# A gated recurrence and an ELU layer: one sum of the weights' rounding as accumulating transfers, and the weight block sums back in an even row

## The chip, the cores and the metric

The kernel runs on one core of a Trainium2 chip. The metric is the device time of one execution in microseconds (us), lower is better. All engines of the core (PE for matrix products, DVE for elementwise work, ACT for activations and copies out of PSUM, POOL, and SP, which only issues transfers) run their own instruction queues in order and meet through semaphores.

## The reference

```python
# q, k, v, a_re, a_im: (4, 8, 768, 48) float32
mag = np.sqrt(a_re * a_re + a_im * a_im)
scale = np.minimum(mag, 0.999) / (mag + 1e-06)
a_re_n, a_im_n = (a_re * scale, a_im * scale)
for t in range(S):                      # one complex gated state per head
    S_re, S_im = a * S_re - b * S_im + kv[t], a * S_im + b * S_re
    y[:, :, t] = np.einsum('bhd,bhde->bhe', q[:, :, t], S_re)
x = y.transpose(0, 2, 1, 3).reshape(3072, 384)
h = x @ w_in                            # (384, 2048), float64 weights
g = np.where(h > 0.0, h, np.exp(np.minimum(h, 0.0)) - 1.0)
return (g @ w_out).astype(np.float32)   # (2048, 384), float64 weights
```

Here `a, b` stand for `a_re_n, a_im_n` of step `t`. The weights arrive as float64, and the kernel rounds them to float32 itself, on the bits.

## The kernel before, in words

The tokens are cut into 12 units of 256 (two batches by 128 steps). A unit goes through the decays (logarithms, angles, exponentials on ACT and DVE), the recurrence as chunked matrix products, a small regrouping of its result into the layer's input (`seam`, six small transfers `x<-y`), the first layer (w_in) and the second (w_out). Units 0 and 1 compute the layer directly (`inner` L1202, `elu` L1215, `project` L1225). From unit 3 on both layers use fewer products on sums and differences of weight blocks (`mult` L1449, `product` L1299); these block sums are made once on DVE (`summed_in` L1398 for w_in, `combined` L1272 for w_out).

**The order** is written by hand. A list `first` gives the steps of the opening stage one by one. After it, every step has a place on a scale of 16 slots to a unit (`put(at, fn, ...)`), and the steps are issued in order of place. Each engine then works its own queue strictly in that order, so a DVE step put in early delays all DVE steps behind it.

**The weights** are 16 blocks of 768 float32 per partition: `("in", 0)` to `("in", 7)`, which are slices of w_in, 3 rows of 256 per partition, and `("out", 0)` to `("out", 7)`, slices of w_out, 768 in a row. Each is fetched by SP as 768 KB of float64 words into one of two raw buffers and then rounded by five DVE steps. Each entry `(convert,)` of `first` issues one step. The first four are in `_rounded` (L36): two on the high words give a truncated float32 `f` (L40, L43), a third takes the exponent of it into `p` (L46), a fourth scales the low words by that exponent, again into `p` (L50). The fifth is a sum of the two into the weight tile:

```python
        nc.vector.tensor_tensor(out=dst, in0=p, in1=f, op=ALU.add)   # L655
```

`f` and `p` share a ring of two buffers (tag `wt`). The first layer of units 0 and 1 is `inner(u, f)` for f = 0, 2, ..., 14; piece f reads block `("in", f // 2)`. Its PSUM bank comes from a ring of three (tag `mlp`) and becomes free when `elu` (ACT L1219, L1220, then DVE L1221) has read it. `project(u, n, f0, f1)` reads blocks `("out", f0 // 2)` and on.

**Other steps that the change touches.** `carry_back` (L817) fetches a row of turns from DRAM by a POOL transfer, which `carried` (L822, DVE) adds to the angles before the PE product L837 of `turned`. `noted` (L784) takes two DVE reductions for a later check of the inputs. `test_fetch` and `test` (L661, L676) read the weights' high words once more in 48 pieces and reduce each on DVE (L680), for the same check; `verdict` (L1485) and `pronounced` (L1506) conclude it. `product` ends in `done` (L1336), which writes a result tile `o` and sends it out. For units from 4 on there is a DVE step `lengths` (L772) that the PE product L889 waits for, and `slopes` (L780) that ACT's angles (L815) wait for.

Of the kernel before, what the change touches and what calls it, by code (L numbers as in the profile page):

```python
# [16 lines left out]
C = 128  # L17
# [18 lines left out]
def _rounded(nc, w, f, p):  # L36


    lo, hi = w[:, :, 0], w[:, :, 1]
    yield nc.vector.tensor_scalar(  # L40
        out=f, in0=hi, scalar1=LOW, scalar2=3, op0=ALU.bitwise_and, op1=ALU.logical_shift_left
    )
    yield nc.vector.scalar_tensor_tensor(  # L43
        out=f, in0=hi, scalar=TOP, in1=f, op0=ALU.bitwise_and, op1=ALU.bitwise_or
    )
    yield nc.vector.tensor_scalar(  # L46
        out=p, in0=f, scalar1=F32_EXP, scalar2=None, op0=ALU.bitwise_and
    )
    p = p.bitcast(FP32)
    yield nc.vector.scalar_tensor_tensor(  # L50
        out=p, in0=lo, scalar=2.0**-52, in1=p, op0=ALU.mult, op1=ALU.mult
    )
# [453 lines left out]
def kernel(  # L506
# [140 lines left out]
    def rounded(kind, m):  # L647

        w, dst = raw.pop((kind, m))
        f = sb.tile([C, WF * DM], U32, tag="wt", bufs=2, name="wf")  # L650
        p = sb.tile([C, WF * DM], U32, tag="wt", bufs=2, name="wp")
        yield from _rounded(nc, w, f, p)
        n = dst.shape[-1]
        f, p = (x.bitcast(FP32).rearrange("p (b n) -> p b n", n=n) for x in (f, p))
        nc.vector.tensor_tensor(out=dst, in0=p, in1=f, op=ALU.add)  # L655
        done.append((kind, m))
        yield True
# [159 lines left out]
    def carry_back(u):  # L817

        if u in carry and u > 3:
            nc.gpsimd.dma_start(out=flat(nat[u]["e"])[0:1], in_=carry[u])  # L820

    def carried(u):  # L822

        if u in carry:
            row = nat[u]["th"][0:1].rearrange("p n h d -> p (n h d)")
            nc.vector.scalar_tensor_tensor(
                out=row, in0=carry[u] if u < 4 else flat(nat[u]["e"])[0:1], scalar=float(2 * np.pi), in1=row, op0=ALU.mult,
                op1=ALU.add,
            )
# [469 lines left out]
    def product(u, k, h):  # L1299
# [36 lines left out]
        def done(i, n, a, *sums):  # L1336
            if u < NU - 1:
                o = new("o", 2, [C, HN])
            else:
                o = flat(new("S", 8, [C, 1, H, D]))[:, 0:HN]  # L1340
# [28 lines left out]
    def A(r, k):  # L1369

        if r == "t":
            return spare[1][:, ds(12 * C, 4 * C)]
# [23 lines left out]
    ] + SUMS[11:] + [(("t", 0), (1, 1), MINUS, 5)]  # L1396
# [52 lines left out]
    def mult(u, p):  # L1449
# [3 lines left out]
        a = four(A(*(("t", 0) if p == 6 and u == PAIRED + 1 else IN_OF[p])))  # L1453
# [31 lines left out]
    def verdict():  # L1485
# [17 lines left out]
        nat[0]["fit"] = t = work([1, NU + NR])  # L1503
        nc.tensor.matmul(t, lhsT=ones, rhs=fit, start=True, stop=True)

    def pronounced():  # L1506
        t = nat[0]["fit"]
# [62 lines left out]
    def decays_of(u, *at):  # L1570
        fns = squares, joined, logarithms, powers, lengths, ratios, slopes, noted, angles, carried
        if u > 3:
            put(at[4] + 0.05, carry_back, u)
# [4 lines left out]
    def gates_of(u, *at):  # L1578
# [8 lines left out]
        (joined, 0, 0), (squared, "ai", 1), (joined, 0, 1), (logarithms, 0, 0),  # L1587
        (logarithms, 0, 1), (fetch, "in", 1), (fetch, "in", 2), (ratios, 0, 0), (lengths, 0, 0),
        (warm, 2), (warm, 1), (lengths, 0, 1), (sums, 1), *2 * [(convert,)],
        (table, "exp_and_others"), (ratios, 0, 1), (powers, 0, 0), (powers, 0, 1), (warm, 2),  # L1590
        (sums, 0), (warm, 1), (angles, 0, 0), (angles, 0, 1), (summed, 0), (summed, 1),
        (decayed, 0, 0), (turned, 0, 0), (decayed, 0, 1), (turned, 0, 1), (waves, 0, 0),
        (waves, 0, 1), (begun, 1), (warm, 1), (scaled, 0, "q", 0), (ends, 0), (scaled, 0, "k", 0),
        (scaled, 0, "k", 1), (scaled, 0, "q", 1), (warm, 1), (gated, 0, 0), (warm, 1), (noted, 0),
        (table, "natural_log"), (warm, 2), (gated, 0, 1), (warm, 2), *3 * [(convert,)],
        (transposed, 0, "k", 0), (transposed, 0, "q", 1), (carry_on, 0), (transposed, 0, "q", 0),
        *4 * [(convert,)], (scores, 0, 0), (transposed, 0, "k", 1), (scores, 0, 1), (load_a, 1),
        (squares, 1), (joined, 1), (fetch, "in", 3), (logarithms, 1), (states, 0, 0),
        (values, 0, 0), (powers, 1), (convert,), (states, 0, 1), (lengths, 1), (load_qk, 1),
        (convert,), (ratios, 1), (values, 0, 1), (seam, 0), (warm, 2), (warm, 2), (decays, 1),  # L1600
        (load_a, 2), (warm, 1), (inner, 0, 0), *2 * [(convert,)], (noted, 1), (scaled, 1),
        (warm, 4), (convert,), (load_v, 1), (slopes, 1), (ends, 1), *3 * [(convert,)],
        (inner, 0, 2), (elu, 0, 0), (convert,), (fetch, "in", 4), (angles, 1), (turns, 1),
        (waves, 1), (gated, 1, 0), (inner, 0, 4), (gated, 1, 1), (transposed, 1, "q", 0),
        (transposed, 1, "k", 0), (convert,), (scores, 1, 0), (load_v, 2), (convert,),
        (fetch, "in", 5), *2 * [(convert,)], (transposed, 1, "k", 1), (states, 1, 0), (convert,),
        (inner, 0, 6), (fetch, "in", 6), (elu, 0, 2), *4 * [(convert,)], (transposed, 1, "q", 1),
        (scores, 1, 1), (fetch, "in", 7), (values, 1, 0), (states, 1, 1), (values, 1, 1),
        (convert,), (seam, 1), *4 * [(convert,)], (inner, 0, 8), (inner, 0, 10), (elu, 0, 4),
        *2 * [(convert,)], (elu, 0, 6), (elu, 0, 8), (fetch, "out", 0), (warm, 2), (inner, 1, 0),  # L1610
        (convert,), (inner, 0, 12), (convert,), (inner, 1, 2), *3 * [(convert,)], (inner, 1, 4),
        (fetch, "out", 1), (fetch, "out", 2), (fetch, "out", 3), (elu, 0, 10), (convert,),
        (inner, 0, 14), (elu, 1, 0), *3 * [(convert,)], (elu, 0, 12), (fetch, "out", 4),
        *3 * [(convert,)], (elu, 1, 2), (inner, 1, 6), *2 * [(convert,)], (fetch, "out", 5),
        (elu, 1, 4), *3 * [(convert,)], (elu, 0, 14), *3 * [(convert,)], (elu, 1, 6),
        (begun, 2), (squares, 2), *2 * [(convert,)], (inner, 1, 8), (inner, 1, 10), (joined, 2),
        (convert,), (inner, 1, 12), (fetch, "out", 6), (fetch, "out", 7), *2 * [(convert,)],
        (elu, 1, 8), (convert,), (project, 0, 0, 0, 4), (convert,), (elu, 1, 10),
        *3 * [(convert,)], (elu, 1, 12), (load_qk, 2), *4 * [(convert,)], (inner, 1, 14),
        (elu, 1, 14), (logarithms, 2), (powers, 2), *4 * [(convert,)], (project, 1, 0, 0, 4),  # L1620
        (project, 1, 1, 0, 4), *3 * [(convert,)], (noted, 2), (lengths, 2), (ratios, 2),
        (slopes, 2), (load_a, 3), (angles, 2), (carried, 2), (convert,), (project, 0, 1, 0, 4),
        (convert,), (project, 0, 0, 4, 8), *3 * [(convert,)], (decays, 2), (project, 1, 0, 4, 8),
        *2 * [(convert,)], (project, 1, 1, 4, 8), (turns, 2), *2 * [(convert,)],
        (project, 0, 1, 4, 8), (begun, 3), (squares, 3), *2 * [(convert,)],
        (project, 1, 0, 8, 12), (waves, 2), (scaled, 2), (joined, 3), (gated, 2), (ends, 2),
        (load_qk, 3), (logarithms, 3), (powers, 3), (project, 1, 1, 8, 12),
        (states, 2, 0), (project, 1, 0, 12, 16), (transposed, 2, "q", 0), (lengths, 3),
        (ratios, 3), (project, 0, 0, 8, 12), (transposed, 2, "k", 0), (transposed, 2, "q", 1),
        (slopes, 3), (angles, 3), (project, 1, 1, 12, 16), (transposed, 2, "k", 1),  # L1630
        (carried, 3), (scored, 2), (turns, 3), (project, 0, 1, 8, 12), (valued, 2), (seam, 2),
        (noted, 3), (project, 0, 0, 12, 16), (opened,), (waves, 3), (summed_in, 0),
        (summed_in, 1), (combined, 1, 0), (combined, 2, 0), (summed_in, 2), (combined, 1, 1),
        (combined, 4, 0), (combined, 2, 1), (scaled, 3), (combined, 4, 1), (ends, 3),
        (project, 0, 1, 12, 16),
    ]
    def layer_of(u, at_h, at_p):
# [33 lines left out]
        if u > NU - 3:  # L1671
            ks[-4:] = (3, 0), (7, 0), (7, 1), (3, 1)
# [7 lines left out]
    for u in range(2, NU):  # L1680
# [7 lines left out]
        else:  # L1688
            sq = (r + 7.2, r + 9.6) if u < PAIRED + 4 else (r + 5.08, r + 6)
            noting = r + (15.7 if u != PAIRED + 2 else 17.6)  # L1690
# [20 lines left out]
    for n in range(11):  # L1711
        put(37 + 0.6 * n, summed_in, n)
    for n, at in (
        (21, 45), (20, 46.5), (11, 49.3), (12, 49.4), (13, 49.5), (16, 50.2), (14, 54.3),
        (15, 55.1), (17, 56), (18, 57), (19, 59.5),
    ):
        put(at, summed_in, n)
    for m, x in enumerate(((1, 0), (2, 0), (1, 1), (4, 0), (2, 1), (4, 1), (3, 0), (3, 1))):
        put(37.2 + m * 0.6, combined, *x)
    clear = [SLOTS * n + x for n in range(3, NU) for x in (0.55, 5.2, 7.35, 9.7, 12.3, 14.2)]  # L1720
    clear = [x for x in clear if x > 57]
    for m in range(NR):
        put(clear[m - 1] + 0.01 if m else 55, test_fetch, m)
        put(clear[m], test)
    assert clear[NR - 1] < NU * SLOTS - 8
    put(NU * SLOTS - 7.5, verdict)
    put(NU * SLOTS - 5, pronounced)
# [40 lines left out]
```

## Time and profile before

| what | value |
|---|---|
| median of 3 runs | 670.95 us (669.23 to 671.93) |
| the profiled execution's own time | 669.23 us |
| its span, first to last instruction | 667.1 us |
| PE busy | 639.6 us, 96% of the span |
| DVE busy | 503.6 us, 75% |
| ACT busy | 419.2 us, 63% |
| POOL busy | 154.4 us, 23% |
| DMA traffic | 56.12 MB, mean 84 GB/s |
| granted PE clock, mean | 0.993 |

The profile is of one execution. Busy shares are means over stages with different limits: the opening stage (to about 130 us, weights being rounded), a passage to the steady order (to about 250 us), the steady order of about 50 us to a unit (to about 600 us), and the end. PE's busy time counts matrix products that flow one behind the other, so what matters is where PE stands idle and what it waits for there.

### The profile page before, as it was taken

To read this page: it belongs to the slowest core of one execution; us is meant where nothing else is said; L and a number is where in the kernel's file an instruction comes from. 1 tells how busy PE (TensorE), PEld (TensorE's weight loads), DVE (VectorE), ACT (ScalarE), POOL (GpSimd) and SP (SyncE) were. 2 spreads that over 40 slices of the span, in tenths; PEclk is the share of its full clock that TensorE was granted. 3 is DMA by queue.
4 is the path that set the end of the run, shared out by engine and by line. 5 is a ranking of instruction groups with operands and counts; after the bars stand their busy time and mean duration, and the time that the engine had idled before them with its cause. 6 is when DMAs were issued, how large, how long until landed. Compare 5 with 4: busy or idle time off the path is not lost.

```text
span 667.1 us, 17231 instructions
## 1 busy us (share of the span) xinstructions
PE 639.6 (96%) x7236; PEld 579.6 (87%) x7236; DVE 503.6 (75%) x801; ACT 419.2 (63%) x684; POOL 154.4 (23%) x200
## 2 busy tenths in 40 slices
PE   8899899999999899999999999999999999999995
PEld 6777786576898798998998998999999999999995
DVE  5889999968777788678678768768768768765481
ACT  6885455874846567667677677677677577471250
POOL 2000000112124303503503503503603602402000
PEclk9799999999999999999999999999999999999999
DMA  9986645630900632452451451451551551212100
GB/s 166 189 142 105 148 149 167 112 72 20 154 3 15 115 56 62 81 106 57 86 106 53 90 104 48 97 104 44 100 104 44 102 104 43 54 32 61 34 2 29
DMA packets 151443, 56.12 MB, mean 84 GB/s; under 512 B 129684, under 2 KB 143164, under 8 KB 151356
## 3 DMA queue, kind: packets, MB, share of 16 engines
q1 hardware_dynamic: 147616, 53.58, 38.8%
q0 software_dynamic: 3520, 1.20, 1.5%
q8 instruction: 59, 0.97, 0.6%
q14 instruction: 28, 0.23, 0.1%
q10 hardware_dynamic: 220, 0.14, 0.1%
HBM read 48.91 MB, written 4.80 MB: 81 GB/s over the span
## 4 chain that ended last, share of the span: by engine, by line
PE 44%; DVE 10%; ACT 8%; issue 3%; DMA 1%; SPq 0%; ACTq 0%; DVEq 0%
PE mlp L1319 18%; PE mlp L1455 10%; PE y L1455 5%; DVE g L1471 3%; PE w L1023 3%; DVE g L1480 3%; PE y L1109 2%; ACT ee L1477 2%; ACT ee L1476 2%; PE w L1064 2%; PE w L837 2%; DVE g L1297 1%; ACT L735 1%; DVE n L772 1%; ACT n L746 1%
## 5 line engine op out<-in xcount | busy, mean ns | idle before, releaser
L1319 PE MATMUL mlp<-w_out,g 128*128 128x192 f32 x640 | 111.8, 328 | 1.0 <-DVE ee L1331 1.0
L1319 PEld LDWEIGHTS mlp<-w_out,g 128*128 128x128 f32 x640 | 104.2, 190 | 4.4 <-DVE ee L1331 1.6
L1081 POOL TENSOR_TENSOR S<-S,T 128x384 f32<-128x384 f32 x36 | 30.9, 857 | 175.5 <-DVE S L1079 175.5
L1210 PE MATMUL mlp<-x,w_in 128*128 128x256 f32 x288 | 65.1, 381 | 3.0 <-DVE g L1221 2.6
L1210 PEld LDWEIGHTS mlp<-x,w_in 128*128 128x128 f32 x288 | 53.8, 190 | 11.7 <-DVE g L1221 3.1
L1471 DVE TENSOR_TENSOR g<-g,mlp 128x512 f32<-128x512 f32 x45 | 30.7, 682 | 40.1 <-ACT qt L1024 28.7
L1297 DVE TENSOR_TENSOR g<-g 128x512 f32<-128x512 f32 x80 | 54.4, 695 | 5.0 <-PE mlp L1319 3.8
L1455 PE MATMUL mlp<-x,w_in 128*128 128x128 f32 x424 | 56.2, 275 | 0.4 <-DVE o L1344 0.4
L1480 DVE SCALAR_TENSOR_TENSOR g<-ee,g 128x512 f32<-128x512 f32 x63 | 47.6, 755 | 11.1 <-ACT ee L1477 11.0
L1319 PE MATMUL mlp<-w,g 128*128 128x192 f32 x320 | 54.5, 329 | 0.0
L1319 PEld LDWEIGHTS mlp<-w,g 128*128 128x128 f32 x320 | 51.8, 190 | 0.6
L1455 PEld LDWEIGHTS mlp<-x,w_in 128*128 128x128 f32 x424 | 51.6, 192 | 0.8 <-DVE o L1344 0.6
L1476 ACT ACTIVATE ee<-g 128x512 f32<-128x512 f32 x63 | 39.5, 627 | 17.2 <-DVE g L1471 16.7
L1190 POOL DMA_DIRECT2D x<-y x62 | 29.8, 488 | 87.2 <-ACT y L1126 37.3
L1468 ACT COPY g<-mlp 128x512 f32<-128x512 f32 x36 | 21.1, 586 | 44.0 <-PE mlp L1455 43.7
L1477 ACT ACTIVATE ee<-ee 128x512 f32<-128x512 f32 x72 | 45.4, 631 | 2.3
L1024 ACT COPY qt<-w 128x512 f32<-128x512 f32 x48 | 25.8, 589 | 15.5 <-PE w L1023 15.4
L973 ACT ACTIVATE cs<-n 128x768 f32<-128x768 f32 (+1 forms) x14 | 10.5, 751 | 38.0 <-DVE n L845 37.9
L904 ACT ACTIVATE n<-w 64x384 f32<-64x384 f32 (+1 forms) x60 | 28.1, 486 | 8.9 <-PE w L889 8.3
L1455 PE MATMUL mlp<-x,g 128*128 128x128 f32 x224 | 29.7, 275 | 1.2 <-DVE o L1344 1.2
L1219 ACT ACTIVATE ee<-mlp 128x512 f32<-128x512 f32 x24 | 14.3, 595 | 25.6 <-PE mlp L1210 17.2
L1455 PE MATMUL y<-x,w_in 128*128 128x128 f32 x216 | 29.0, 277 | 1.4 <-ACT g L1468 1.4
(222 smaller groups left out, 1434.8 us busy)
## 6 DMA issues: line engine op xcount, KB each, us to landing
w<-in_moe_w_out_dram SPq DMA_DIRECT2D x8, 768.0 KB
g<-in_moe_w_in_dram SPq DMA_DIRECT2D x24, 256.0 KB
g<-in_moe_w_out_dram SPq DMA_DIRECT2D x24, 256.0 KB
w<-in_moe_w_in_dram SPq DMA_DIRECT2D x16, 288.0 KB
vn<-in_v_dram SPq DMA_DIRECT2D x24, 192.0 KB
ar<-in_a_re_dram SPq DMA_DIRECT2D x22, 192.0 KB
ai<-in_a_im_dram SPq DMA_DIRECT2D x22, 192.0 KB
q<-in_q_dram SPq DMA_DIRECT2D x22, 192.0 KB
```

The source lines that it names most:

```text
L904: nc.scalar.activation(out=flat(x[key][to, n : n + 1]), in_=t[of], func=AF.Exp, scale=sign)
L1024: nc.scalar.copy(out=o[:, h0 : h0 + 4], in_=t)
L1081: eng.tensor_tensor(out=new_s, in0=new_s, in1=wide, op=ALU.mult)
L1190: eng.dma_start(out=x["x"][ds(j * HP + D, G), i], in_=x["y"][ds(j * HP + i * G, G)])
L1210: nc.tensor.matmul(t[:, e], lhsT=w_in[:, i, ts(f + e, C)], rhs=x["x"][:, i], start=(i == 0), stop=(i == NI - 1),)
L1297: nc.vector.tensor_tensor(out=S_of(u, k, h), in0=a, in1=b, op=op)
L1319: nc.tensor.matmul(to, lhsT=a[:, m], rhs=b[:, m], start=(first and h == 0 and m == 0), stop=False, skip_group_check=True,)
L1455: nc.tensor.matmul(x["c" + c][:, ts(m, C)], lhsT=a[:, m], rhs=x["mix"][p], start=(p == BANKS[c][0] and m == 0), stop=False, skip_group_che ...
L1471: nc.vector.tensor_tensor(out=part(u, to), in0=part(u, a), in1=part(u, b), op=op)
L1476: nc.scalar.activation(out=e, in_=part(u, of), func=AF.Relu, scale=-1.0)
L1477: nc.scalar.activation(out=e, in_=e, func=AF.Exp, scale=-1.0)
L1480: nc.vector.scalar_tensor_tensor(out=part(u, to), in0=nat[u]["e", to], scalar=-1.0, in1=part(u, of), op0=ALU.add, op1=ALU.max,)
```

## The change

The last step of the rounding changes for 14 of the 16 blocks, all but `("in", 0)` and `("in", 1)`. `f` is now built in place in the weight tile, and the sum is a transfer within SBUF, issued from POOL, that adds `p` onto it. A converted block takes four entries `(convert,)` instead of five, so entries are dropped from `first`; the pieces `(inner, 0, 6)`, `(inner, 0, 10)`, `(inner, 0, 12)` and `(inner, 0, 14)` come some entries later among what surrounds them. On PE's own queue only one of these is seen: `(inner, 0, 12)` now stands behind `(inner, 1, 2)`.

In the built program, DVE's step L46 of a block waits for the accumulating transfer of the block two before it, whose buffer `p` it takes, and the first PE product of a piece waits for the transfer of its block.

The rest of the diff puts other steps elsewhere: the last ten block sums of w_in in an even row from place 45.4 (a separate block `t` for one of them goes away), two of `combined` to 46 and 47, `noted` of unit 4 to 20.3 instead of 17.6 behind its base, `carry_back` behind `slopes` and into another buffer, the 48 tests at even distances of 2.5 slots, the verdict in one piece among the last products, the results of the last unit in the ring `o` of two buffers, and the order of the last two units' products like that of the others.

```diff
 def rounded(kind, m):
         w, dst = raw.pop((kind, m))
-        f = sb.tile([C, WF * DM], U32, tag="wt", bufs=2, name="wf")
         p = sb.tile([C, WF * DM], U32, tag="wt", bufs=2, name="wp")
-        yield from _rounded(nc, w, f, p)
-        n = dst.shape[-1]
-        f, p = (x.bitcast(FP32).rearrange("p (b n) -> p b n", n=n) for x in (f, p))
-        nc.vector.tensor_tensor(out=dst, in0=p, in1=f, op=ALU.add)
+        if kind == "in" and m < 2:
...
+        else:
+            n = dst.shape[-1]
+            p = p.rearrange("p (b n) -> p b n", n=n)
+            each = _rounded(
+                nc, w.rearrange("p (b n) two -> p b n two", n=n), dst.bitcast(U32), p
+            )
+            for _ in range(3):
+                yield next(each)
+            for _ in each:
+                pass
+            nc.gpsimd.dma_start(out=dst, in_=p.bitcast(FP32), accum_op=ALU.add)
         done.append((kind, m))
         yield True
...
-            nc.gpsimd.dma_start(out=flat(nat[u]["e"])[0:1], in_=carry[u])
+            nc.gpsimd.dma_start(out=flat(nat[u]["w"])[0:1], in_=carry[u])
...
-            if u < NU - 1:
-                o = new("o", 2, [C, HN])
-            else:
-                o = flat(new("S", 8, [C, 1, H, D]))[:, 0:HN]
+            o = new("o", 2, [C, HN])
...
-    ] + SUMS[11:] + [(("t", 0), (1, 1), MINUS, 5)]
+    ] + SUMS[11:]
...
-            put(at[4] + 0.05, carry_back, u)
+            put(at[6] + 0.3, carry_back, u)
...
-        if u > NU - 3:
-            ks[-4:] = (3, 0), (7, 0), (7, 1), (3, 1)
...
-            noting = r + (15.7 if u != PAIRED + 2 else 17.6)
+            noting = r + (15.7 if u != PAIRED + 2 else 20.3)
...
-    for n in range(11):
-        put(37 + 0.6 * n, summed_in, n)
-    for n, at in (
-        (21, 45), (20, 46.5), (11, 49.3), (12, 49.4), (13, 49.5), (16, 50.2), (14, 54.3),
-        (15, 55.1), (17, 56), (18, 57), (19, 59.5),
-    ):
-        put(at, summed_in, n)
+    for n in range(len(SUMS)):
+        put(37 + 0.6 * n if n < 11 else 45.4 + 0.6 * (n - 11), summed_in, n)
...
-        put(37.2 + m * 0.6, combined, *x)
-    clear = [SLOTS * n + x for n in range(3, NU) for x in (0.55, 5.2, 7.35, 9.7, 12.3, 14.2)]
-    clear = [x for x in clear if x > 57]
+        put(37.2 + m * 0.6 if m < 6 else 40 + m, combined, *x)
     for m in range(NR):
-        put(clear[m - 1] + 0.01 if m else 55, test_fetch, m)
-        put(clear[m], test)
...
-    put(NU * SLOTS - 7.5, verdict)
-    put(NU * SLOTS - 5, pronounced)
+        put(54 + 2.5 * m, test_fetch, m)
+        put(56 + 2.5 * m, test)
+    put(NU * SLOTS, verdict)
```

## The prediction

> **What bounds the kernel now.** I read the page first (span, engine shares, clock row), then the table of windows by stage, then PE's timeline with the releasers of its gaps, then DVE's timeline, and last the landings of transfers.
>
> ```profile
> PE 639.6 (96%) x7236; PEld 579.6 (87%) x7236; DVE 503.6 (75%) x801; ACT 419.2 (63%) x684; POOL 154.4 (23%) x200
> 45.00:60.00 15.00, 13.49 (x128) 11.21 (x127) 13.45 (x22) 8.94 (x14) 0.48 (x1) 1.00 0.76 134
> 60.00:76.00 16.00, 12.69 (x289) 10.81 (x289) 14.94 (x23) 7.94 (x19) 1.44 (x3) 1.00 0.69 125
> 76.00:104.00 28.00, 26.58 (x125) 23.13 (x125) 27.41 (x39) 13.86 (x23) 0.00 (x0) 1.00 0.51 151
> 104.00:130.00 26.00, 26.00 (x90) 15.67 (x91) 24.40 (x33) 18.69 (x26) 0.00 (x0) 1.00 0.67 153
> 130.00:196.00 66.00, 65.74 (x766) 51.64 (x765) 48.74 (x63) 42.28 (x71) 13.98 (x17) 1.00 0.35 63
> ```
>
> The columns are the window, its length, busy time of PE, PEld, DVE, ACT and POOL, the granted clock, the DMA share and GB/s. DVE is nearly full from 45 to 130, which invites relief, but PE is full too: of the 85 us it idles about 6.2. From 104 on it has nothing to gain before 196. So fewer DVE steps shorten the kernel only through PE's gaps before 104:
>
> ```profile
> 55.44 1.09 PE L1023 MATMUL w<-ident,qg 128*128 128x128 f32 x8 [0.92 <-DVE qg L1003]
> 61.31 2.86 PE L1210 MATMUL mlp<-x,w_in 128*128 128x256 f32 x12
> 69.11 0.81 PE L1100 MATMUL y<-a,vn 64*64 64x64 f32 x32 [0.37 <-DVE a L1036]
> 70.43 2.86 PE L1210 MATMUL mlp<-x,w_in 128*128 128x256 f32 x12
> 75.94 2.86 PE L1210 MATMUL mlp<-x,w_in 128*128 128x256 f32 x12 [2.65 <-DVE g L1221]
> 103.98 0.59 PE L1235 MATMUL mlp<-w_out,g 128*128 128x384 f32 x1 [1.42 <-DVE g L1221]
> ```
>
> Each row gives start, duration, and in brackets the idle time before it with its releaser. The four bracketed gaps sum to 5.4 us.
>
> **What the opening stage gains.** Fourteen sums (L655) go, at 0.95 to 0.96 us each: 13.3 us of DVE time. By gap:
> - 0.92 before L1023: its DVE step stands behind L842, which waits for PE's own product L837 at 51.5. One sum ahead of it goes, but that wait absorbs most: I take 0.2.
> - 0.37 before L1100: gone.
> - 2.65 at 75.94: the releaser is the DVE step of `elu(0, 4)`, and that step waited for ACT:
>
> ```profile
> 71.13 2.73 ACTq L1190 DMA_DIRECT2D x<-y  x3
> 73.91 0.60 ACT L1219 ACTIVATE ee<-mlp 128x512 f32<-128x512 f32 x1 [2.81 <-issue]
> 75.20 0.69 DVE L1221 SCALAR_TENSOR_TENSOR g<-ee,mlp 128x512 f32<-128x512 f32 x1 [0.47 <-ACT ee L1220]
> ```
>
> ACT issues three `seam` transfers for 2.73 us before it can start the exponential. DVE even idled 0.47 there. The change leaves ACT's order alone, so this gap stays.
> - 1.42 at 103.98: DVE's own queue was late. Gone.
>
> Gain: 0.2 + 0.37 + 1.42 = 2.0 us.
>
> **What it costs there.** A piece of `inner` now waits for a transfer to land, where it waited for 0.95 us of DVE. Nothing in this trace accumulates, and none moves 384 KB within SBUF, so I bound the landing. From below: the small POOL transfers `x<-y` land 1.7 us after issue at the least; `T<-ends` (1536 pieces) lands in 3.9 to 4.0, so 384 pieces add about (3.95 - 1.7) x 384 / 1536 = 0.6; 384 KB at the rate of the fullest window (151 GB/s at a share of 0.51 is 296 GB/s when alone; 125 at 0.69 is 181) takes 1.3 to 2.2, say 1.5. Sum 3.8. From above: an accumulation reads both sides, so 3.0 for the data, and a busy stage disturbs (`x<-y` took up to 4.1 at 71 us against 1.7): 1.7 + 0.6 + 3.0 + 2.4 = 7.7. I take 5.0, nearer the lower end, as the DMA share is 0.7 and not 1.
>
> Block ("in", 3) serves `inner(0, 6)`. Its last DVE step now:
>
> ```profile
> 57.91 0.95 DVE L50 SCALAR_TENSOR_TENSOR wp<-w,wp 128x768 f32<-128x768 uint32 x1
> 59.58 0.95 DVE L655 TENSOR_TENSOR w_in<-wp,wf 128x768 f32<-128x768 f32 x1
> ```
>
> L50 ends at 58.86, after the change at about 58.65. PE stands ready at 61.31 - 0.2 = 61.1, so 2.4 us of landing are covered by other products. At 5.0 PE waits 58.65 + 5.0 - 61.1 = 2.5 us (1.35 at 3.8, 5.25 at 7.7). Block ("in", 5) for `inner(0, 10)` ends L50 at 72.15 and PE wants it at about 75.9 plus the first wait: I take 1.6 for a second wait, since POOL's queue there also holds three `x<-y` of `seam(1)` (1.44 us of issue), within 0.4 to 4.4. Block 2 lands at 45.6 + 5 = 50.6 against 51.77 where PE wants it; blocks 4, 6 and 7 and those of w_out lie further ahead: nothing.
>
> New wait on DVE: L46 of a block waits for the transfer of the block two before. Behind it on DVE stand the `elu` steps L1221, which free PSUM banks for PE. The ring's cycle is two pieces of PE work, 2 x 5.2 us, less 1.5 of DVE steps: landings up to 8.9 us cost nothing.
>
> DVE's shapes: for the six w_in blocks L40 and L46 now read or write 3 x 256 views. They may keep 0.56 us or fall to 0.95 as the two-source steps do: 12 x 0.39 = 4.7 us of DVE at most. L849, on 8 rows of 48, takes 0.36 where L842 of the same 128x384 takes 0.55, so a split shape kept its pace there; I take 0.
>
> The Trainium skill, "VectorE: DVE Perf Modes", section "What auto-detection actually checks", would have L46 lose the fast form: it wants source and destination in SBUF with outermost dimensions both even or equal, and 3 against 768 is neither. By it alone 6 x 0.39 = 2.3 us of DVE would come back in the w_in stage; no row of this trace shows an odd split.
>
> Also on the page of "SBUF — State Buffer", the box on the trap "DVE blocks DMA" speaks against the change: a POOL-issued transfer cannot have its descriptors written while DVE runs a two-port operation. The nearest row is POOL's `more<-n` at 54.41, issued in 0.48 while DVE's L849 ended, with no visible delay. By the rule I estimate one L40 (0.56 us) onto each landing, so the first wait would be 3.1 and not 2.5.
>
> Opening: -2.0 + 2.5 + 1.6 = **+2.1**; with both waits at the low end -2.0 + 1.35 + 0.4 = -0.25, at the high end -2.0 + 5.25 + 4.4 = +7.7.
>
> **The passage (196 to 250).** PE idles 3.95 us here. In unit 4 DVE gets five sums (0.6 each) and two `combined` (0.87 each), 4.74 us, between `lengths` and `carried`:
>
> ```profile
> 209.58 0.95 DVE L826 SCALAR_TENSOR_TENSOR n<-n 1x768 f32<-1x768 f32 x1 [2.11 <-ACT n L815]
> 210.67 1.53 PE L837 MATMUL w<-n,sum_turns 128*128 128x384 f32 x4
> ```
>
> DVE idled 2.11 there, so `carried` is 2.6 late, and PE, ready at 210.58, stalls 2.6. Given back: idle of 1.23 at 217.4 and of 0.42 and 0.45 near 224, whose releasers had queued behind the sums that now are earlier, and some 0.6 at 236 to 248, where two sums (0.68, 0.60) leave DVE's chain. Net **-0.1**, bounds -0.3 to +1.4.
>
> **The steady units.** PE idles 0.41 us a unit. `carry_back` behind `slopes` lands at about 313.7 (311.4 + 0.54 + 1.7 to 2.3), `carried` starts at 315.01: 1.1 us of cover, so 0; without the cover its shortfall would fall on L837. Tests cost 0.33 each wherever they stand; before, one lay on DVE's chain per unit, after it is none or one or two: **0**, bounds -1 to +1 over seven units.
>
> **The end.** In the last two units (7, 0) follows (6, 1) at once and waits for two `elu` results, 0.36 + 0.40 + 0.08 = 0.85 where the profile has 0.52: 2 x 0.33 = 0.66. Verdict reductions (0.29) leave the chain near 641. The ring of two `o` is free 1.74 us after issue, before it is needed, and the verdict lies in DVE's idle 4.48 us at 654.7: **+0.4**.
>
> Sum: 2.1 - 0.1 + 0 + 0.4 = +2.4 against the profiled execution, whose own time is 669.23 (span 667.1 and 2.13 around it): 671.6. The median of the runs is 1.72 above that execution, so 673.3.
>
> **Rivals.**
> - Hidden landing: if transfers land within about 2.4 us, or PE arrives later than I think, both waits vanish and -2.0 stays. Then -2.0 - 0.1 + 0.4 = -1.7 and 669.2; 666.6 if the 2.65 goes as well, should the later pieces reorder what ACT meets first. For it: small POOL transfers land in 1.7. Against: 384 KB are 24 times the bytes of an `x<-y`.
> - Slower: landings of 7 to 8 us or more, because SP's fetch of block 5 starts as L50 of block 3 frees its raw buffer, in the same microsecond as the accumulation, at a DMA share of 0.7. Then PE stalls 4.5 us or more before `inner(0, 6)`, and the granted clock drops, as it did after the thin stretch at 16 to 20 us:
>
> ```profile
> 20.00:21.00 1.00, 1.00 (x6) 1.00 (x6) 1.00 (x4) 1.00 (x3) 0.00 (x0) 0.50 1.06 227
> ```
>
>   A clock of 0.50 for 6 us costs 3; +7.7 for the waits gives +8 to +11: 679 to 682. It decides from a landing of about 7 us; past 8.9 each w_out block waits too. Against: the small transfers' rows, which are short of 7 even when disturbed (4.1).
> - It does not free DVE: if the 3 x 256 views run at 0.95, the w_in blocks give back 4.7 of their 5.7 us, the gain of 0.57 in the first gaps is lost, and the time is 674.
>
> **How the numbers follow.** The main case (landing 4 to 6 us, 670 to 676) gets 0.45, of it 0.29 same and 0.16 slower. The hidden landing gets 0.30, half faster, half same. The slow landing gets 0.25. About 0.5%, 667.6 to 674.3, is what a measurement can tell from no change: faster 0.15, same 0.44, slower 0.41. Range 667.5 to 681, from the hidden case to the middle of the slow one.
>
> **What would show it.** Right: L1221's gap at 103.98 gone, the 2.65 kept, a new gap of 2 to 3 us before `inner(0, 6)` released by a DMA, landings of the accumulating transfers near 5 us, L837 of unit 4 late by 2.6. Wrong: landings below 3 or above 7, a clock below 1.00 between 60 and 104, L40 or L46 at 0.95, or DVE idle in 104 to 130 behind L46.

## The result, and the profile after

The changed kernel takes **701.9 us** (699.5 to 704.8 in four runs) where the kernel before took 671.4 beside it: 1.046 times as long, 95% interval 1.0415 to 1.0511. Here and below, a ratio leaves out executions that took over 1.5% longer than the fastest of their kernel. The forecast was 673.3 with a range to 681.0. The profiled execution took 699.51 with a span of 697.8, so 30.7 us were lost against the span before.

The page of the changed kernel: the engine line, the granted clock in 40 slices, and the group of the first layer's products (its last part is PE's idle time ahead of them and what ended it):

```profile
PE 652.1 (93%) x7236; PEld 589.1 (84%) x7236; DVE 494.5 (71%) x786; ACT 419.7 (60%) x684; POOL 172.9 (25%) x214
PEclk9899899989999899999999999999999999999998
L1222 PE MATMUL mlp<-x,w_in 128*128 128x256 f32 x288 | 69.2, 398 | 9.9 <-DMA w_in<-wp 9.9
```

DVE lost 9.1 us of work and POOL got 18.5. PE's busy time grew by 12.5 us although its products are the same. Taken over windows of half a microsecond, PE's busy time times the missing share of its clock is 15.9 us after and 2.9 before, so the growth is products at half clock. A group that waited 2.6 us for DVE now waits 9.9 us for transfers.

The stages, with the columns as in the prediction (clock, DMA share and GB/s last):

```profile
45.00:60.00 15.00, 10.76 (x74) 8.77 (x73) 14.33 (x22) 7.92 (x13) 1.88 (x2) 0.96 1.00 167
60.00:76.00 16.00, 15.23 (x331) 13.13 (x331) 9.89 (x15) 7.81 (x16) 2.54 (x2) 0.93 0.69 112
76.00:104.00 28.00, 22.05 (x103) 18.45 (x100) 19.25 (x26) 10.15 (x19) 6.34 (x7) 0.88 0.84 157
104.00:130.00 26.00, 25.16 (x99) 18.36 (x98) 20.83 (x30) 16.64 (x25) 4.91 (x5) 1.00 0.94 243
```

DVE is less busy (19.25 of 28 us where it had 27.41), in part because its own steps now wait for PE, and PE is the one that stands idle. The DMA share, 0.76, 0.69, 0.51 and 0.67 before, is now 1.00, 0.69, 0.84 and 0.94.

PE's timeline at its large gaps:

```profile
57.46 4.27 PE L1222 MATMUL mlp<-x,w_in 128*128 128x256 f32 x12 [3.94 <-DMA w_in<-wp]
80.43 5.49 PE L1222 MATMUL mlp<-x,w_in 128*128 128x256 f32 x12 [4.05 <-DMA w_in<-wp]
87.82 2.83 PE L1222 MATMUL mlp<-x,w_in 128*128 128x256 f32 x12 [1.90 <-DMA w_in<-wp]
115.24 2.85 PE L1247 MATMUL mlp<-w_out,g 128*128 128x384 f32 x8 [0.84 <-DVE g L1233]
151.87 1.96 PE L1076 MATMUL w<-vn,kg 64*64 64x48 f32 x64 [5.58 <-DVE kg L1015]
234.53 2.90 PE L849 MATMUL w<-n,sum_turns 128*128 128x384 f32 x4 [4.32 <-DVE n L838]
```

The first three are `inner(0, 4)`, `inner(0, 8)` and `inner(0, 10)`, which wait for blocks 2, 4 and 5. The same products before and after show where the 30.7 us went: the first product of w_out starts at 115.24 for 103.98 (11.3 late), the products of the block sums at 217.91 for 198.28 (19.6 late), the log sums at 282.98 for 257.45 (25.5 late), the last stall at 684.97 for 655.15 (29.8 late).

Of the 11.3, 1.6 stood before the first accumulating transfer is issued at 48.34: `inner(0, 0)` starts at 43.31 for 41.70. The granted clock was 0.57 from 38 to 42 us there and 1.00 before; it also fell at about that place in the profiled executions of runs 2 and 12 below (0.50 from 40 to 42), whose opening is that of the kernel before, so I do not count these 1.6 as the change's.

The transfers themselves, from the group of line L667 (POOL's time to issue one in ns, and the landings):

```profile
L667 POOL DMA_DIRECT2D w_out<-wp x8: 849/894/1174, 102.0 to 139.0; - x8
L667 POOL DMA_DIRECT2D w_in<-wp x6: 1257/1276/1336, 48.3 to 92.1; - x6
DMA to landing us min/median/max: 4.8/7.3/9.1
```

### The profile page after: what moved, and what is told of

It is laid out like the page before. It is cut to its first block, busy times and chain, and to the rows that moved or that the text cites. A ratio compares the mean times of both kernels' runs of the same rounds, so it can differ in the third digit from the quotient of the medians.

```text
span 697.8 us, 17236 instructions
## 1 busy us (share of the span) xinstructions
PE 652.1 (93%) x7236; PEld 589.1 (84%) x7236; DVE 494.5 (71%) x786; ACT 419.7 (60%) x684; POOL 172.9 (25%) x214
## 4 chain that ended last, share of the span: by engine, by line
PE 57%; DVE 14%; DMA 11%; ACT 9%; issue 4%; SPq 3%; POOL 0%; DVEq 0%; ACTq 0%; POOLq 0%
PE mlp L1331 18%; PE mlp L1462 10%; PE y L1462 6%; PE mlp L1222 6%; PE w L1035 4%; PE w L1076 3%; PE y L1121 3%; DMA w<-in_moe_w_out_dram 3%; DMA w_in<-wp 3%; SPq L598 3%; DVE g L1478 2%; PE w L849 2%; PE y L1148 2%; DMA w<-in_moe_w_in_dram 2%; DVE g L1487 2%
## 5 line engine op out<-in xcount | busy, mean ns | idle before, releaser
L1331 PEld LDWEIGHTS mlp<-w_out,g 128*128 128x128 f32 x640 | 105.6, 192 | 5.5 <-DVE ee L1344 2.4
L1093 POOL TENSOR_TENSOR S<-S,T 128x384 f32<-128x384 f32 x36 | 33.5, 931 | 189.3 <-DVE S L1091 189.3
L1222 PE MATMUL mlp<-x,w_in 128*128 128x256 f32 x288 | 69.2, 398 | 9.9 <-DMA w_in<-wp 9.9
L1222 PEld LDWEIGHTS mlp<-x,w_in 128*128 128x128 f32 x288 | 56.2, 199 | 20.1 <-DMA w_in<-wp 8.8
L1309 DVE TENSOR_TENSOR g<-g 128x512 f32<-128x512 f32 x80 | 57.7, 731 | 5.1 <-PE mlp L1331 4.0
L1462 PEld LDWEIGHTS mlp<-x,w_in 128*128 128x128 f32 x432 | 52.6, 192 | 0.0
L1487 DVE SCALAR_TENSOR_TENSOR g<-ee,g 128x512 f32<-128x512 f32 x63 | 44.1, 701 | 11.6 <-ACT ee L1484 11.4
L1484 ACT ACTIVATE ee<-ee 128x512 f32<-128x512 f32 x72 | 45.4, 631 | 2.3
L1076 PE MATMUL w<-vn,kg 64*64 64x48 f32 x1280 | 28.7, 225 | 6.3 <-DVE kg L1015 5.6
L1076 PEld LDWEIGHTS w<-vn,kg 64*64 64x64 f32 x1280 | 24.9, 139 | 11.0 <-DVE kg L1015 6.2
```

The source lines that it names most:

```text
L1076: nc.tensor.matmul(to, lhsT=of, rhs=vn[u % 2][ts(c, L), n, ts(h, D)], start=True, stop=True,)
L1093: eng.tensor_tensor(out=new_s, in0=new_s, in1=wide, op=ALU.mult)
L1222: nc.tensor.matmul(t[:, e], lhsT=w_in[:, i, ts(f + e, C)], rhs=x["x"][:, i], start=(i == 0), stop=(i == NI - 1),)
L1309: nc.vector.tensor_tensor(out=S_of(u, k, h), in0=a, in1=b, op=op)
L1331: nc.tensor.matmul(to, lhsT=a[:, m], rhs=b[:, m], start=(first and h == 0 and m == 0), stop=False, skip_group_check=True,)
L1462: nc.tensor.matmul(x["c" + c][:, ts(m, C)], lhsT=a[:, m], rhs=x["mix"][p], start=(p == BANKS[c][0] and m == 0), stop=False, skip_group_che ...
```

## The experiments

**1. The sums back on DVE.** The changed kernel, with the transfer replaced:

```diff
-            nc.gpsimd.dma_start(out=dst, in_=p.bitcast(FP32), accum_op=ALU.add)
+            nc.vector.tensor_tensor(out=dst, in0=p.bitcast(FP32), in1=dst, op=ALU.add)
```

> The changed kernel with the 14 accumulating transfers put back as DVE sums (in place in the weight tile, in the fourth entry), all else as changed. Theory A, the transfers make the opening loss: PE's lag behind the kernel before at the first product of w_out falls from 11.3 us to 3 or less, the half-clock stretches between 50 and 110 us go, only the 10 us lost after 195 us stay: 680 to 686 us. Theory B, the moved pieces and the 3x256 views (12 steps at 0.95 for 0.56, 4.7 us of DVE) make it: still 10 us late at the first product of w_out, 692 us or more.

Measured: 683.7 us, 1.018 of before (1.017 to 1.020). So 18.2 of the 30.5 us are the transfers', although DVE has 13 us more to do without them. The total is as theory A said; the lag is not. PE is still 6.9 us late at the first product of w_out (110.90 for 103.98; 1.0 of it stood at `inner(0, 0)`). Its gaps ahead of that, 2.75, 1.02 and 2.53 us, all wait for DVE's step of `elu`. I read this as the order written for the transfers having no room for 14 sums; no run tests it.

**2 and 3. The two halves of the change.** The opening list and `rounded` of one kernel, with everything else of the other.

> The opening (list and rounding) as in the kernel before, everything behind it as changed. If the parts are separate: no lag to 195 us, then the 6.3 us of unit 4 and 3 to 4 us of the units and the end: 680 to 683 us. If the loss behind 195 us was a consequence of the late opening: 672 us or less.

> The opening as changed, everything behind it as in the kernel before (the complement of the run with the opening of before). Separate parts: 19.6 us late at 195 us and 1 or less after, 689 to 692 us, and the two complements' losses sum to 30 us. If they interact, the sum is off by over 4 us.

Measured: 677.7 us with the opening of before, 1.009 (1.006 to 1.011), 2 short of the expected range; 692.2 us with the rest of before, 1.031 (1.025 to 1.036), at its upper end. In the second, PE is 22.2 us late at 195 us and no later at the end, so the opening's loss is carried unchanged. Losses of 0.9% and 3.1% sum to 4.0%, the whole change cost 4.6%. The sum is 3 us short by the medians and 4.7 by the ratios, where over 4 was to mean an interaction; with intervals of up to half a per cent either side that stays open. Run 1 lies 6.0 above run 2: so much is the changed order of the opening with the sums on DVE.

**4 and 5. Which weights.** Only the eight blocks of w_out by transfers (w_in summed on DVE, in flat tiles), and only the six of w_in (w_out on DVE in place).

> The changed kernel, but the w_in blocks are summed on DVE (flat tiles of 768, in the fourth entry), so only the 8 blocks of w_out use transfers. Theory A1, each stage pays its own landings: no wait before the pieces of the first layer, the 8.3 us lost at 130 to 150 stay: 689 to 692 us. Theory A2, the loss at 130 to 150 is carried from the late w_in stage, since the raw fetches of w_out started 6.5 us late: 680 to 684 us.

> The changed kernel with only the six w_in blocks summed by transfers, the eight of w_out on DVE in place (in the fourth entry). If the two stages pay separately, 18.2 us divide into 6.5 for w_out (the run with only w_out, 690.5, less the run with all sums on DVE, 684.0) and the rest for w_in: 695 to 696 us here. If the loss is one, shared stall, 700 us or more, or below 692.

Measured: 690.5 us (1.030, 1.026 to 1.034) and 694.3 us (1.033, 1.028 to 1.038). Against the runs with all sums on DVE (684.0 flat, 683.7 in place) the w_out transfers cost 6.5 us and those of w_in 10.6 (about 11.7 expected): 17.1 of 18.2. With only w_in, `inner(0, 4)` and `inner(0, 8)` wait 5.19 and 5.76 us for their transfers. With only w_out no piece of the first layer waits for a transfer. PE's timeline, and then ACT's, show this at 130 to 140 us:

```profile
140.53 1.96 PE L1079 MATMUL w<-vn,kg 64*64 64x48 f32 x64 [6.03 <-DVE kg L1018]
```

```profile
129.27 0.84 ACT L724 ACTIVATE n<-ar 128x768 f32<-128x768 f32 x1 [3.35 <-DMA ar<-in_a_re_dram]
133.98 0.84 ACT L725 ACTIVATE n<-ai 128x768 f32<-128x768 f32 x1 [3.86 <-DMA ai<-in_a_im_dram]
```

No PE product waits for a w_out transfer here. The loads of `ar` and `ai` land late, ACT cannot square them, the step `kg` of the recurrence is late, and PE waits 6.03 us. The windows of this run give a DMA share of 1.08 from 116 to 130 us (0.80 before). Run 6, the same order with DVE's sums, has 0.75 there, ACT squares `ar` after a wait of 0.22, and PE has no such gap. So theory A1 holds: w_out pays its own price, through what else the DMA engines carry.

**6. The flat tiles.** The run with the sums on DVE, but rounded in flat tiles of 768.

> As the run with the sums on DVE, but with the rounding in flat tiles of 768 as in the kernel before, in the changed order. If the 3x256 views cost 4.7 us of DVE in the w_in stage: L40 and L46 take 0.56 for all blocks, PE's lag at the first product of w_out falls by 3 to 5 us, 679 to 681 us against 683.7. Rival, that DVE time was covered: 683 to 684 us.

Measured: 684.0 us against 683.7. The views do cost DVE what was feared, as the group of L40 in the changed kernel shows:

```profile
L40 DVE TENSOR_SCALAR w_out<-w x8: 542/558/561, 95.6 to 135.6; 128x768 uint32<-128x768 uint32 x8
L40 DVE TENSOR_SCALAR w_in<-w x6: 941/946/953, 40.8 to 87.9; 128x768 uint32<-128x768 uint32 x6
```

but in that order the time was covered.

**7. The transfer by itself.** Six transfers at the end of the kernel before, each after the one before, with nothing waiting.

> The kernel before with six transfers within SBUF behind the last use of w_in, each after the one before, that nothing waits for: an accumulation of 128 x 768 floats, a plain copy of the same, an accumulation in 3 x 256, then these three again. If the 7.3 us median landing of the changed kernel is the transfer's own price, the quiet accumulations take 6.5 us or more; if it is the contention of that stage, 3.5 to 5 us, as the prediction's lower end says. If accumulating is what costs, the copy is shorter than the accumulation by 1 us or more.

Measured (ns to issue, and landings; L1568 accumulates, twice flat and twice in 3 x 256; L1566 is the plain copy):

```profile
L1568 POOL DMA_DIRECT2D w_in<-w_in x4: 924/1096/1297, 637.3 to 657.1; - x4
DMA to landing us min/median/max: 4.0/4.5/6.1
L1566 POOL DMA_DIRECT2D w_in<-w_in x2: 571/573/575, 641.7 to 654.2; - x2
DMA to landing us min/median/max: 2.6/2.6/2.6
```

The flat accumulations landed in 4.0 and 4.2 us, those in 3 x 256 in 4.8 and 6.1. Accumulating costs 1.4 to 1.6 us over copying. Of the 7.3 of the changed kernel some 4 to 6 are thus the transfer's own; the rest I put down to the other traffic of that stage.

**8. The traffic by itself.** The kernel before with all its DVE sums, and six accumulating transfers added beside the first six blocks of w_out (plus four copies of 192 KB).

```diff
+        if kind == "out" and m < 6:
+            nc.gpsimd.dma_start(
+                out=w_out[:, ts(6 + m % 2, WF)], in_=w_out[:, ts(0, WF)], accum_op=ALU.add
+            )
```

> The kernel before, all its DVE sums kept, with six accumulating transfers of 384 KB added beside the first six blocks of w_out, into blocks of w_out that are rounded later and so overwritten (and four plain copies of 192 KB that fill them first); only POOL and the late rounding of those two blocks meet them. Theory D, the traffic delays the raw fetches and the loads behind them on SP: the loads of q, k, ar, ai take up to 5 us longer, PE stalls before the product of vn and kg near 136 us, 675 to 679 us. Rival, the loss came from the waits for landings (DVE's L46, PE's pieces) and not from the traffic: 672 us or less.

Measured: 673.9 us, 1.0043 (1.0022 to 1.0065), 3.0 over before and 1 short of theory D's range. The stall is not where I expected it, at the loads, but one step earlier: DVE's L40 waits 2.44 us for a raw block (0.4 and 0.3 for two others), `lengths` is late, and PE waits 2.60 before the log sums at 126.8; its gap at the first product of w_out is 2.82 for 1.42. SP ends the raw fetches at 121.1 where before it was 114.0 (1.9 of these 7.1 us stood already at the first block of w_out). The profiled execution took 677.8, 3.9 over the median, so its rows overstate the loss. The two waits, on DVE and on PE:

```profile
117.10 0.58 DVE L40 TENSOR_SCALAR wf<-w 128x768 uint32<-128x768 uint32 x1 [2.44 <-DMA w<-in_moe_w_out_dram]
126.84 0.88 PE L899 MATMUL w<-n,sum_logs 64*64 64x384 f32 x8 [2.60 <-DVE n L782]
```

The traffic alone costs time with no consumer waiting for it; late rounding of the two blocks used as targets may be part of it.

**9 and 10. The clock.** Unused products ahead of the two pieces that waited 4 us.

> The changed kernel with 28 extra 128x128 products of the identity on PE's queue ahead of each of the two pieces that wait 4 us for a transfer, inner(0, 4) and inner(0, 8); their results are unused, nothing waits for them. Theory C, the half clock follows PE's idle stretch: the half-clock stretches at 58.7 and 79.2 us (3.4 and 6.9 us long) go, PE's lag at the first product of w_out falls from 11.3 us by up to half of them, 3 to 5 us: 697 to 699 us. Rival, the clock falls for the load of the stage and not for the idle stretch: it falls again, 701 us or more.

> As the run with filled waits, but 15 products (3.4 us by the 0.115 us that the trace of that run gives for each half of one) instead of 28, so that they end before the transfer lands. Theory C, the half clock follows idle and costs time: inner(0, 4) takes 2.86 and not 4.27 us and starts when its transfer lands; 1.4 us at least, up to 3 of the 11.3 us of lag at the first product of w_out go: 695 to 700 us. Rival, the later landings set the lag, whatever the clock: lag 11.3 again, 700 us or more.

Measured: 1.038 of before (1.032 to 1.044; three executions, 693.3 to 699.7 us) with 28 products, 1.042 (1.038 to 1.047; three, 696.4 to 703.1) with 15, against 1.046 (1.0415 to 1.0511) for the change. Windows of the changed kernel, then of the run with 28 products:

```profile
59.00:62.00 3.00, 3.00 (x10) 2.35 (x9) 1.26 (x2) 0.00 (x0) 1.29 (x1) 0.50 0.54 117
80.00:86.00 6.00, 5.49 (x12) 3.87 (x12) 4.41 (x6) 1.27 (x4) 1.69 (x2) 0.50 1.17 201
```

```profile
50.00:60.00 10.00, 10.00 (x73) 9.18 (x72) 9.63 (x15) 2.67 (x5) 0.54 (x1) 1.00 0.87 143
76.00:86.00 10.00, 8.46 (x76) 8.01 (x71) 7.55 (x10) 2.89 (x7) 4.17 (x5) 1.00 1.15 192
```

The half clock is gone where PE does not idle, with the DMA share as high as before (1.15 for 1.17): at these two places it follows the idle stretch and not the load. But the first product of w_out starts at 115.27 with the filling and 115.24 without: 28 products ran 2.4 and 3.4 us past the two landings. What the clock alone cost is not settled, as the three intervals overlap.

**11. The block sums back in their places.** The kernel of run 2, with `summed_in` and `combined` where they were before.

> The kernel of the run with the opening of before, with the places of the block sums and of the two combined steps put back too (tests one place later, so that block t is free for them). If the sums ahead of carried make the loss of unit 4: the stall of 4.3 us before the product of sum_turns in unit 4 goes, 674 us; 2.5 to 3.5 us over before stay from tests, verdict and product order. Rival, the changed landing place of carry_back makes it: 677 us.

Measured: 674.5 us, 1.006 (1.004 to 1.009). The stall of 4.3 us in unit 4 is gone, as PE's row in run 2 and then here shows:

```profile
216.61 2.90 PE L837 MATMUL w<-n,sum_turns 128*128 128x384 f32 x4 [4.30 <-DVE n L826]
```

```profile
211.09 1.53 PE L837 MATMUL w<-n,sum_turns 128*128 128x384 f32 x4
```

The remaining 0.6% stay for what is still changed behind the opening: tests, verdict, product order, the ring `o` and the place of `carry_back`, which makes no stall there by itself.

**12. The neighbour on POOL.** The kernel of run 2, with POOL's product k x n of unit 4 later.

> The kernel of the run with the opening of before, with POOL's product k x n of unit 4 put behind POOL's carry transfer, so that it no longer runs beside DVE's carried. If that step's 2.6 us (0.95 before) came from running beside the POOL product: it takes 0.95 again, the stall of 4.3 us is 2.6, 675.5 to 676.5 us. Rival, it is slow for the new place of its row: 2.6 again, 677.7 us.

DVE's and POOL's timelines, first of the changed kernel (the same stall as in run 2), then of this run with PE's row last:

```profile
231.76 2.62 DVE L838 SCALAR_TENSOR_TENSOR n<-n 1x768 f32<-1x768 f32 x1
```

```profile
231.75 1.81 POOL L994 TENSOR_TENSOR k<-k,n 128x768 f32<-128x768 f32 x1
```

```profile
215.29 0.94 DVE L826 SCALAR_TENSOR_TENSOR n<-n 1x768 f32<-1x768 f32 x1
219.53 3.27 DVE L1398 TENSOR_TENSOR w_in<-w_in,g 128x512 f32<-128x512 f32 x2
```

```profile
220.41 1.83 POOL L982 TENSOR_TENSOR k<-k,n 128x768 f32<-128x768 f32 x1
216.37 2.06 PE L837 MATMUL w<-n,sum_turns 128*128 128x384 f32 x4 [2.64 <-DVE n L826]
```

`carried` takes 0.94 again and PE's stall is 2.64 us, as the expectation put it. But the time is 677.9, the same as run 2. The POOL product now runs beside two block sums, which take 3.27 us where they took 1.28, and PE waits 0.32 us for DVE at 229.62. That does not use up the gain: from the products of the block sums around 200 us to the same ones of the next unit, run 2 takes 58.46 us (200.01 to 258.47) and this run 57.16 (201.44 to 258.60), 1.3 less. This execution came there 1.4 later, out of its opening, at a clock near 0.50 from 37 to 43 us. Four executions of each (675.8 to 679.5 and 675.9 to 678.5) do not tell 1.3 us from nothing.

**13 to 16. Is a covered transfer free?** In the kernel before, only the first three blocks of w_out were summed by transfers. The first try also moved `seam(1)`'s three ACT issues to POOL.

> The kernel before with two edits at its two largest waits between 60 and 104 us: the sums of the first three blocks of w_out by accumulating transfers, and the three x<-y of seam(1) that ACT issued issued by POOL. If a transfer is free where its landing (7 us) is covered and the traffic is light: PE's gap of 1.42 at the first product of w_out goes; the gap of 2.65 falls to 1 or less with ACT freed; 667 to 668 us against 670.9. Rival, three transfers beside the raw fetches already give it back: the same as before or slower, 671 us or more.

Measured: 675.7 us, 1.0062 (1.0042 to 1.0082). DVE's timeline names the cause:

```profile
101.31 0.56 DVE L40 TENSOR_SCALAR wf<-w 128x768 uint32<-128x768 uint32 x1 [1.43 <-DMA w_out<-wp]
106.21 0.56 DVE L46 TENSOR_SCALAR wp<-wf 128x768 uint32<-128x768 uint32 x1 [2.60 <-DMA w_out<-wp]
```

Block 3 takes both buffers of the ring for its `f` and `p`, so DVE stands still until the transfers of blocks 1 and 2 have read theirs, and `elu` L1228 behind it is late: PE waits 3.62 at the first product of w_out. The next runs build `f` in the weight tile for all of w_out, so that the ring holds `p` alone; one has this alone, one has `seam(1)` on POOL with `elu(0, 4)` two entries earlier, one has both.

> The kernel before; the blocks of w_out are rounded in place (f in the weight tile), the first three summed by transfers, the other five on DVE. No step of DVE now waits for a landing of the block just before. If a covered landing is free: the gap of 1.42 at the first product of w_out goes, 669 to 670 us against 670.9. If the traffic alone costs (0.5 us a transfer by the run with six added): 671.5 to 672.5. If DVE's wait was not what cost: 675 us again.

> The kernel before, without any transfer of the change: the three x<-y of seam(1) that ACT issued are issued by POOL, and elu(0, 4) stands two entries earlier. If the gap of 2.65 us was ACT's 2.73 us of issues: it falls below 1, 668.5 to 669.5 us. Rival, x lands later from one queue and the later piece of unit 1 waits: 671 us.

> Both edits of the two runs before it. If they are separate: the sum of their two differences; 667 to 669 us if both gain.

Measured: 672.2 us (1.0009, 0.998 to 1.004), 672.0 us (1.0005, 0.998 to 1.003), and for both **668.8 us, 0.9957 (0.9930 to 0.9985)**, the fastest kernel of the study. Two rows of the PE timeline of the last:

```profile
74.34 2.86 PE L1220 MATMUL mlp<-x,w_in 128*128 128x256 f32 x12 [0.51 <-DVE g L1231]
102.61 1.56 PE L1245 MATMUL mlp<-w_out,g 128*128 128x384 f32 x4
```

The gap of 2.65 is 0.51 here, followed by 0.81 and 0.17; the gap of 1.42 before w_out is gone. With the seam edit alone that second gap grew to 2.02: what one gap gave, the next took until DVE had been relieved too. The two edits are not separate, as their own differences sum to +0.14% and both together give -0.43%: the forecast of 667 to 669 came true although neither gained alone. The transfers alone removed the gap at w_out, and the profiled execution was 2 us shorter than that of before, but the medians do not tell it from no change.

## Why the prediction was wrong, step by step

The sum was +2.4 us and the profiled execution lost 30.7. The step that failed is **What it costs there**: the transfers were priced at two waits, 4.1 us, and all else of them at nothing; run 1 puts them at 18.2, of which runs 4 to 6 show 10.6 for w_in and 6.5 for w_out. The passage, the units and the end, +0.3 together, were some +11 in the profiled execution (run 2 puts them at 6.6 by the medians).

- **What DVE's relief can buy**: PE was the bound, and 13 us of DVE steps could return at most PE's gaps; nothing speaks against that. Of the 2.0 us, the gaps before L1023 and L1100 went (0.92 and 0.37 to under 0.2), but PE came to them after its wait of 3.94, so that does not show DVE's relief. The one before w_out shrank only from 1.42 to 0.84. That the 2.65 us gap was ACT's issues was right in part: with ACT freed and `elu` earlier (run 15) it became 1.8 in three pieces.
- **The landing, taken as 5.0, was 7.3 (4.8 to 9.1)**, with the w_in blocks at 7.0 to 9.1, four of the six beyond the upper bound of 7.7. The lower bound, 3.8, was near the quiet price of a flat transfer, 4.0 to 4.2. The working put too little on contention (2.4 at most, from a 16 KB transfer) and nothing on POOL's longer issue (0.85 to 1.3 us for 0.48) or on the 3 x 256 pieces. The trap of the Trainium skill's page "SBUF — State Buffer" that I weighed, DVE holding up POOL's descriptors, is not seen in POOL's issue, which took 0.85 to 1.34 us in the full stage and 0.92 to 1.30 in the quiet one.
- **"Block 2 lands at 50.6: nothing"** failed first: its L50 ended at 48.03 (1.6 of the 2.4 us stood before, 0.8 are L40 and L46 at 0.95) and PE was ready at 53.52, so a landing of 5.0 would still have been in time. It took 9.1, and `inner(0, 4)` waited 3.94 us. That delayed PE past block 3's landing, so no wait stood at `inner(0, 6)`, where I had put the first; blocks 4 and 5 gave 4.05 and 1.90. Sum 9.9 for the 4.1 of the forecast. The dependence on every block was in the text; only blocks 3 and 5 got a wait.
- **"w_out lies further ahead: nothing"** failed by 6.5 us (runs 4 and 6). I priced the wait for the landing, which indeed never came, and not the load on the DMA engines: raw fetches and the loads of unit 3 came late, and DVE and ACT passed that on to PE.
- **DVE's wait for a buffer** did not decide in the changed kernel: no row there has DVE wait for an accumulating transfer. The mechanism is real, as run 13 shows, where the ring was shared.
- **The 3 x 256 views**: taken as 0, they cost 0.39 x 12 of DVE's time. The Trainium skill's rule ("VectorE: DVE Perf Modes", "What auto-detection actually checks") spoke for L46 to slow down; the trace agrees (0.95 us for 0.56). L40 I had read as 3 against 3, which the rule would let stay fast, and the trace has it slow as well (946 ns for 558). The rows of its source lie evenly spaced in one run, as those of `p` do, so it may count as 768 too; no row shows the shapes that DVE was given. The rows that I leaned on, the DVE steps L849 and L842 of the kernel before, differ in more than the shape: the first reads SBUF, the second PSUM. Run 6 shows no cost in time without the transfers.
- **The passage, -0.1, was +5.9** (19.6 to 25.5 late). My 2.6 us for `carried` is the 2.64 of run 12. Missing were the 1.67 us by which POOL's product stretched `carried`, and the half clock: behind the stall the product L849 took 2.90 us for 1.53, and behind a gap of 1.96 at 256.57 (1.39 before) the clock was 0.50 from 257 to 260.
- **Steady units, 0, were some 3.4**, from 25.5 late to the 29.3 at which the first stall of the end stands, less the 0.4 that this stall grew. I counted 0.33 us of busy time to a test and not its wait for its own fetch. DVE's timeline after:

```profile
506.91 0.42 DVE L692 TENSOR_REDUCE seen<-g 128x1 f32<-128x256 f32 x1 [3.17 <-DMA g<-in_moe_w_out_dram]
507.25 1.47 DVE L1478 TENSOR_TENSOR g<-g,mlp 128x512 f32<-128x512 f32 x2
```

  The test holds DVE until its data lands, and the layer's step behind it starts late: PE waits 1.01 at 511.55, and 1.66 at 613.67 behind another. Seven of the 48 tests waited so, 13.5 us of DVE in all; before, none did. This is read from the trace; no run undid the tests alone.
- **The end, +0.4**, was +1.7: two stalls of 0.91 for 0.52 give 0.8, and the span ends 0.9 later behind them. I had called the ring of two `o` free before it is needed; DVE's last step waits for it:

```profile
691.57 0.36 DVE L1353 TENSOR_TENSOR o<-mlp,ee 128x192 f32<-128x192 f32 x1 [2.67 <-DMA out_dram<-o]
```

- **The rival that came true** was the slower one, in part: landings past 7 us and a half clock behind PE's stalls. Its price was short, because it too left out the second stage, the passage and the units, and its place was off: the stalls stood at `inner(0, 4)` and `inner(0, 8)`, and none at `inner(0, 6)`.

## What to carry to other kernels

A step that moves from a full engine to a transfer is paid three times: its landing under the traffic of that very stage (here nearly twice the quiet one), the DMA time that it takes from the loads behind it, and the buffers that it holds; so price each consumer by itself, and then the loads that nobody changed. The same idea used for three blocks with 7 us of cover and no buffer shared gained nothing that twelve executions show; with the neighbouring gap closed as well, both gained 0.4%. Fourteen blocks with the order written around them lost 4.6%, of which the transfers are 18.2 us or 2.7%.

## What the runs showed of the hardware that was not expected

- An accumulating transfer within SBUF costs more than a copy of the same 384 KB: 4.0 to 4.2 us against 2.6 when quiet, and POOL needs 0.92 us to issue it against 0.57.
- A DVE step and a POOL product side by side lengthen the DVE step: 2.62 us for 0.95 beside a POOL product of 1.81, and in run 12 3.27 for 1.28.
- With PE's four idle stretches of 3.9 to 5.6 us in the changed kernel came 3 to 7 us at a clock of about 0.50. The Trainium skill, "TensorE: Matmul & The Clock Gate", "Why this matters for your kernels", asks for no idle gap over about 3 us. These rows agree, but shorter gaps were followed by a drop too: 2.64 us in run 12 by a mean clock of 0.57 from 217 to 221 us, 1.96 us in the changed kernel by 0.50 from 257 to 260. The 2.65 us gap of the kernel before was not followed by any (1.00 from 76 to 84), and the drop at 38 to 42 us of the changed kernel had no single gap over 0.6 us in the 14 us ahead of it.
